# Keys of attention in three tiles of 128, with the left 64 of two head pairs worked in quarters of the array

## The chip, the cores and the metric

One core of a Trainium2 chip. The metric is the device time of one execution, in microseconds (us). Every kernel was run several times, alternating with the kernel before on the same chip.

In lines of the profile PE is TensorE (PEld its weight loads), DVE VectorE, ACT ScalarE, POOL GpSimd and SP SyncE; L486 is line 486 of that run's kernel; `[1.36 <-DVE ...]` is the idle time before an instruction and what ended it. PSUM is the memory where this kernel's products land; its tiles are banks of it, and a bank is written anew only after its last content was copied out. "Half clock" means a granted TensorE clock of 0.5.

## The reference, cut to what matters

```python
# q, k, v: (8 batches, 12 heads, 448 rows, 64)
q_n, k_n = rmsnorm(q, g_q), rmsnorm(k, g_k)
scores = (1 / 8) * q_n @ k_n.T                # 448 x 448 per head
attn = softmax(scores)
x = attn @ v                                  # bridged to (3584, 768)
h = x @ w_in                                  # 768 -> 2048
out = (h * sigmoid(h)) @ w_out                # 2048 -> 768, all float32
```

## The kernel before

Heads are taken in pairs, 48 pairs in all; a pair's 2 x 64 head columns fill 128 partitions. The 448 keys are cut into four tiles of 112. Scores have keys on partitions, so `e` needs no transpose for the weighted sums. Feed-forward products of finished batches are filled in between (`fill`), in two stretches per pair. Each batch of six pairs is an outer index `b`; feed-forward work starts small with the second batch and in full with the third.

```python
def transpose(n, name):                        # q shown; k alike, copied into kT times the gains
    t = ps.tile([P, S], F32, name="tr")        # one PSUM bank
    for j in range(J):                         # J = 4
        nc.tensor.transpose(t[:, ts(j, R)], rows[:, j, :], ident[0:R, 0:R])     # R = 112
    nc.scalar.copy(qT[n % 2], t)

def scores(n, half):
    for j in range(2 * half, 2 * half + 2):
        banks = ps.tile([P, 2, BANK], F32, name="sc", bufs=2)[0:R]
        for h in range(2):
            rows = ds(h * D, D)
            nc.tensor.matmul(banks[:, h, 0:S], kT[rows, ts(j, R)], qT[n % 2][rows, :], ...)
        for h in range(2):
            nc.scalar.activation(e[j][:, h, :], banks[:, h, 0:S], AF.Exp, scale=...)

def weigh(n, half):                            # for its two tiles and both heads
            nc.tensor.matmul(st["av"][ds(h * D, D), :], st["v"][:, h, j, :], e[j][:, h, :], ...)

def add_up(n, *chunks):                        # sum of e over tiles, for the row sums
    for j in chunks:
        nc.vector.tensor_tensor(out=t, in0=e[0] if j == 1 else t, in1=e[j], op=ALU.add)

for n in range(last + 2):                      # cut
    load(n + 3, "qk")
    scores(n, 0)
    weigh(n - 1, 1); load(n + 1, "v"); add_up(n - 1, 2, 3); unload(n - 1)   # ScalarE copies "av" out
    transpose(n + 1, "q")
    fill()
    divide_by_sums(n)                          # row sums, reciprocal, transfers
    scores(n, 1)
    weigh(n, 0)
    transpose(n + 1, "k")
    add_up(n, 1)
    fill()
    weights_in(n, 3)                           # queues two weight loads of 512 KB in the first 12 pairs
    normalise(n + 3)
```

## Time and profile before

| | |
|---|---|
| time, median (first runs) | 1458.72 us (1457.11 to 1459.0) |
| TensorE busy | 1429.4 of 1457.2 us |
| VectorE, ScalarE, GpSimd busy | 708.3, 540.4, 397.9 us |
| 13th pair's q transposes start | 126.1 us |
| from the 28th to the 48th pair's q transposes | 383.1 us |

The lines of the profile that carry this are in the prediction. The last two rows are marks: the first record of a pair's q transposes stands in every kernel's trace, so the times between two marks compare stretches. 126.1 us is the end of the stretch with little feed-forward work; from the 28th to the 48th pair the work repeats evenly, ten double pairs long.

### The profile page before, as it was taken

The page shows a single profiled execution, that of the slowest core. Times are in us where ns is not written, and L with a number is a line of the kernel's source. Part 1 is how long each engine was busy: PE and PEld are TensorE (multiplying, and loading weights), DVE is VectorE, ACT ScalarE, POOL GpSimd, SP SyncE. Part 2 cuts the span into 40 slices and gives each one's busy share as a digit, 9 for nine tenths or more (in the row PEclk, how much of TensorE's full clock was granted, in tenths as well). Part 3 has the DMA queues.
Part 4 walks back from the last instruction along what each step waited for, and adds up shares of the span by engine and source line. Part 5 has one row for each costly group of instructions (what it writes and reads, how often), then busy time and mean ns, then how long its engine had stood idle before and what let it go on. Part 6 is the DMA issues. An engine that isn't in the chain of part 4 may idle for free.

```text
span 1457.2 us, 14067 instructions
## 1 busy us (share of the span) xinstructions
PE 1429.4 (98%) x5057; PEld 699.0 (48%) x5057; DVE 708.3 (49%) x941; ACT 540.4 (37%) x907; POOL 397.9 (27%) x251
## 2 busy tenths in 40 slices
PE   8999999999999999999999999999999999999998
PEld 4333443434444444444444445555555555555554
DVE  5888776765645445654545687722222222222220
ACT  7876566645465465555555344300000000000000
POOL 6565443533323333333322054310000000000000
PEclk9999999999999999999999999999999999999999
DMA  6633344422232232223221167332222222222210
GB/s 188 174 93 112 91 127 134 126 67 73 64 98 74 61 105 67 70 67 99 68 66 66 58 181 246 123 98 78 83 83 80 81 81 83 80 85 84 85 58 25
DMA packets 124052, 137.67 MB, mean 94 GB/s; under 512 B 50372, under 2 KB 104644, under 8 KB 123972
## 3 DMA queue, kind: packets, MB, share of 16 engines
q1 hardware_dynamic: 123904, 136.62, 31.2%
q8 instruction: 42, 0.69, 0.2%
q14 instruction: 38, 0.31, 0.1%
q10 hardware_dynamic: 68, 0.05, 0.0%
HBM read 88.47 MB, written 41.29 MB: 89 GB/s over the span
## 4 chain that ended last, share of the span: by engine, by line
PE 84%; DVE 3%; DMA 1%; issue 1%; ACT 1%; POOL 0%; SPq 0%; ACTq 0%; DVEq 0%; POOLq 0%
PE mm L539 38%; PE sc L539 13%; PE sc L413 8%; PE av L429 8%; PE av L539 7%; PE tr L539 7%; PE tr L457 1%; PE tr L399 1%; PE tr L394 1%; DVE work L461 1%; DVE work L441 1%; DMA hidden<-stage 0%; DMA W<-in_moe_w_in_dram 0%; DVE rms L309 0%; DVE W L490 0%
## 5 line engine op out<-in xcount | busy, mean ns | idle before, releaser
L418 ACT ACTIVATE work<-sc,rms 112x448 f32<-112x448 f32 x384 | 211.9, 636 | 185.7 <-PE sc L413 149.3
L539 PE MATMUL mm<-x,W 128*128 128x448 f32 x648 | 261.0, 542 | 1.2 <-DVE stage L490 1.1
L315 POOL TENSOR_TENSOR rms<-rms,minus_half 112x16 f32<-112x16 f32 (+1 forms) x49 | 176.3, 3599 | 255.5 <-DVE rms L311 254.8
L539 PE MATMUL mm<-sums_x,W 128*128 128x448 f32 x480 | 194.6, 542 | 2.7 <-DVE parts L490 1.8
L413 PE MATMUL sc<-work 64*112 64x448 f32 x768 | 172.4, 568 | 2.2 <-ACT work L403 0.8
L539 PEld LDWEIGHTS mm<-x,W 128*128 128x128 f32 x648 | 118.6, 190 | 107.6 <-issue 98.4
L429 PE MATMUL av<-work,rows 112*64 112x448 f32 x768 | 165.6, 552 | 0.0
L441 DVE TENSOR_TENSOR work<-work 112x896 f32<-112x896 f32 x144 | 157.9, 1097 | 1.8
L559 POOL TENSOR_TENSOR parts<-parts,stage 128x448 f32<-128x448 f32 (+1 forms) x37 | 42.2, 1139 | 336.4 <-DVE parts L490 336.4
L539 PEld LDWEIGHTS mm<-sums_x,W 128*128 128x128 f32 x480 | 88.0, 190 | 81.7 <-issue 72.3
L413 PEld LDWEIGHTS sc<-work 64*112 64x112 f32 x768 | 61.7, 174 | 104.6 <-issue 78.5
L429 PEld LDWEIGHTS av<-work,rows 112*64 112x64 f32 x768 | 46.7, 136 | 106.6 <-issue 100.1
L559 POOL TENSOR_TENSOR parts<-parts,W 128x384 f32<-128x384 f32 x9 | 8.9, 994 | 307.5 <-DVE parts L490 307.5
L461 DVE RECIPROCAL work<-tr 128x448 f32<-128x448 f32 x25 | 73.9, 2956 | 37.6 <-PE tr L457 37.5
L490 DVE TENSOR_TENSOR stage<-mm,parts 128x448 f32<-128x448 f32 (+1 forms) x59 | 36.3, 616 | 86.0 <-PE mm L539 57.0
L546 ACT COPY stage<-mm 128x448 f32<-128x448 f32 (+1 forms) x34 | 17.8, 524 | 155.7 <-PE mm L539 146.0
L670 ACT ACTIVATE stage<-stage 128x896 f32<-128x896 f32 x64 | 58.4, 945 | 36.7 <-DVE stage L490 35.7
L539 PE MATMUL mm<-W,work 128*128 128x384 f32 x204 | 68.6, 486 | 0.0
L539 PE MATMUL sc<-W,work 128*128 128x384 f32 x192 | 64.5, 486 | 0.0
L405 DVE TENSOR_SCALAR work<-tr,gains 128x448 f32<-128x448 f32 x36 | 24.6, 684 | 73.7 <-PE tr L399 73.7
L309 DVE TENSOR_REDUCE rms<-qn 112x8 f32<-112x512 f32 x49 | 33.4, 682 | 48.9 <-ACT qn L308 48.8
L319 POOL TENSOR_TENSOR qn<-rows,rms 112x512 f32<-112x512 f32 x46 | 55.1, 1198 | 3.6
(158 smaller groups left out, 1789.5 us busy)
## 6 DMA issues: line engine op xcount, KB each, us to landing
hidden<-stage SPq DMA_DIRECT2D x64, 448.0 KB, 2.8
work<-hidden SPq DMA_DIRECT2D x7, 2048.0 KB, 9.3
x<-hidden SPq DMA_DIRECT2D x7, 2048.0 KB, 8.8
W<-in_moe_w_in_dram SPq DMA_DIRECT2D x24, 512.0 KB, 4.7
rows<-in_moe_w_out_dram SPq DMA_DIRECT2D x32, 384.0 KB, 3.5
rows<-in_q_dram SPq DMA_DIRECT2D x48, 224.0 KB, 3.5
rows<-in_k_dram SPq DMA_DIRECT2D x48, 224.0 KB, 4.2
rows<-in_v_dram SPq DMA_DIRECT2D x48, 224.0 KB, 2.7
```

The lines of the kernel that those rows point to most:

```text
L309: nc.vector.tensor_reduce(out=rms[:, i], in_=t, axis=AX.X, op=ALU.add)
L315: nc.gpsimd.tensor_tensor(out=flat, in0=flat, in1=half, op=ALU.pow)
L319: engine.tensor_tensor(out=by_head, in0=rows["q"], in1=factor, op=ALU.mult)
L413: nc.tensor.matmul(banks[:, h, 0:S], kT[rows, ts(j, R)], qT[n % 2][rows, :], start=True, stop=True,)
L418: nc.scalar.activation(e[j][:, h, :], banks[:, h, 0:S], AF.Exp, scale=rms[n % 4][:, 1, h, j : j + 1])
L429: nc.tensor.matmul(st["av"][ds(h * D, D), :], st["v"][:, h, j, :], e[j][:, h, :], start=(j == 0), stop=(j == J - 1),)
L441: nc.vector.tensor_tensor(out=t, in0=e[0] if j == 1 else t, in1=e[j], op=ALU.add)
L461: nc.vector.reciprocal(out=r[0], in_=t)
L490: nc.vector.tensor_tensor(out=out, in0=a, in1=b, op=ALU.add)
L539: nc.tensor.matmul(t, self.left(name, s), self.right(name, s), start=s == ends[0], stop=s == ends[1])
L559: nc.gpsimd.tensor_tensor(out=u2, in0=u2, in1=p5, op=ALU.add)
L670: nc.scalar.activation(t, t, AF.Silu)
```

## The change

Three tiles of 128 keys instead of four of 112 leave 64 keys of each head. Those of an even pair and of the odd pair after it share one tile. Its four products (two pairs, two heads) have 64 rows and 64 columns each, so they fit the four quarters of the array at once, for scores and for weighted sums. For this the loads of k and v are split, the weighted sums of two pairs need two PSUM banks at once ("end0" and "end1", which also take the transposes and row sums in turn), and odd iterations do the weighted sums before their scores.

```diff
+    def scores(n, *units):
+        for j in units:
+            banks = ps.tile([P, 2, BANK], F32, name="sc", bufs=2)
+            members = [n] if j < LEFT else [n, n + 1]
+            size = P // len(members)
+            for i, m in enumerate(members):
+                for h in range(2):
+                    rows = ds(h * D, D)
+                    nc.tensor.matmul(banks[ds(i * size, size), h, 0:S],
+                        kT[rows, ds(j * P + i * size, size)], qT[m % 2][rows, :], ...)
 ... (cut)
+    def add_up(n, *units):
+        for j in units:
+            rows = ds(0, P) if j < LEFT else ds(n % 2 * z.LEFT, z.LEFT)
+            nc.vector.tensor_tensor(out=t[rows], in0=e[0] if j == 1 else t[rows], in1=e[j][rows], ...)
 ... (cut; the loop)
-        if n <= last:
-            scores(n, 0)
+        if n <= last and (n < 2 or not odd):
+            scores(n, 0, 1)
         if n > 0:
-            weigh(n - 1, 1)
+            weigh(n - 1, LEFT - 1)
+            if odd:
+                weigh(n, LEFT)
             load(n + 1, "v")
-            add_up(n - 1, 2, 3)
+            add_up(n - 1, LEFT - 1)
+            if odd:
+                add_up(n - 1, LEFT)
             unload(n - 1)
+        if n > 1 and odd:
+            scores(n, 0, 1)
 ... (cut: transpose q, fill, divide_by_sums)
-            scores(n, 1)
+            scores(n, LEFT - 1)
+            if n > 0 and not odd:
+                scores(n, LEFT)
 ... (cut)
-            weigh(n, 0)
+            weigh(n, 0, 1)
 ... (cut: transpose k)
             add_up(n, 1)
+            if odd:
+                add_up(n, LEFT)
```

More of the change, by code (lines that the diff above doesn't have):

```diff
@@ L43, in __init__ @@
         self.REST = self.S - self.FULL * self.P
+        self.KEYS = self.S // self.P
+        self.LEFT = self.S - self.KEYS * self.P
+        assert 2 * self.LEFT == self.P and self.NPAIR % 2 == 0
         assert 2 * self.D == self.P and self.J * self.R == self.S and 2 * self.REST == self.P
@@ L204 @@
     ring = const.tile([P, 7 * n], F32, name="rows")
-    slots = [ring[0:R, ds(i * n, n)] for i in range(7)]
+    slots = [ring[:, ds(i * n, n)] for i in range(7)]
     rings = {"q": slots[0:2], "k": slots[2:5], "v": slots[5:7]}
@@ L217, in load, with load_plain @@
         for name in names:
-            order = "p j h d" if name == "k" else "p h j d"
             t = rings[name][n % len(rings[name])]
-            t = t.rearrange(f"p ({order[2:]}) -> {order}", h=2, j=J)
-            nc.sync.dma_start(
-                t, sources[name][b, ts(hp, 2)].rearrange(f"h (p j) d -> {order}", j=J)
-            )
-            state[n][name] = t if name != "k" else t.rearrange("p j h d -> p h j d")
+            source = sources[name][b]
+            if name == "q":
+                t = t[0:R].rearrange("p (h j d) -> p h j d", h=2, j=J)
+                nc.sync.dma_start(t, source[ts(hp, 2)].rearrange("h (p j) d -> p h j d", j=J))
+                state[n][name] = t
+                continue
+            size = z.KEYS * 2 * D
+            if name == "k":
+                main = t[:, 0:size].rearrange("p (j h d) -> p j h d", j=z.KEYS, h=2)
+                order = "p j h d"
+            else:
+                main = t[:, 0:size].rearrange("p (h j d) -> p h j d", h=2, j=z.KEYS)
+                order = "p h j d"
+            keys = source[ts(hp, 2), 0 : z.KEYS * P].rearrange(f"h (p j) d -> {order}", j=z.KEYS)
+            nc.sync.dma_start(main, keys)
+            state[n][name] = t if name == "k" else main
+            if hp % 2 == 0:
+                left = t[:, ds(size, 2 * D)].rearrange("p (h d) -> p h d", h=2)
+                for i in range(2):
+                    rest = source[ts(hp + i, 2), z.KEYS * P : z.S].rearrange("h p d -> p h d")
+                    nc.sync.dma_start(left[ds(i * z.LEFT, z.LEFT)], rest)
+                state[n][name + "left"] = left
+    def load_plain(state, n):
+        b, hp = pairs[n]
+        for name in "qkv":
+            t = rings[name][n % len(rings[name])][0:R]
+            t = t.rearrange("p (h j d) -> p h j d", h=2, j=J)
+            nc.sync.dma_start(t, sources[name][b, ts(hp, 2)].rearrange("h (p j) d -> p h j d", j=J))
+            state[n][name] = t
     load(state, 0, "qk")
     load(state, 1, "qk")
-    g1 = const.tile([1, 2, D], F32, name="g1")
+    room = Room(nc, const, w_in, z)
+    g1, both = (
+        room.rest[0:1, ds(room.rest.shape[1] - (i + 1) * 2 * D, 2 * D)].rearrange(
+            "p (two d) -> p two d", two=2
+        )
+        for i in range(2)
+    )
     gains = const.tile([P, 1], F32, name="gains")
@@ L233 @@
         nc.scalar.dma_start(g1[:, i, :], g.rearrange("(one d) -> one d", one=1))
-    room = Room(nc, const, w_in, z)
     for n in range(2):
@@ L248 @@
     most = const.tile([1, 1], F32, name="most")
-    both = const.tile([1, 2, D], F32, name="both")
     wide = [g1[:, i : i + 1, :].to_broadcast([1, 2, D]) for i in range(2)]
@@ L274 @@
     normal = [const.tile([R, J, 2, D], F32, name=f"qn{i}") for i in range(2)]
-    rms = [const.tile([R, 2, 2, J], F32, name=f"rms{i}") for i in range(4)]
-    normalise_rows(
-        nc, z, state[0], normal[0], normal[1].rearrange("p j h d -> p h j d"), rms[0], minus_half,
-        nc.vector, together=False,
-    )
+    rms = [const.tile([P, 4 * J], F32, name=f"rms{i}") for i in range(4)]
+    for t in rms:
+        nc.gpsimd.memset(t, 1.0)
+    spare = const.tile([P, 2 * J * D], F32, name="squares")
+    normalise_rows(nc, z, state[0], normal[0], spare, rms[0], minus_half, nc.vector, together=False)
     def arm():
         own = [dict(st) for st in state]
+        plain = [dict() for st in state]
         r = copy.copy(room)
@@ L287, in arm @@
             tc=tc, nc=nc, z=z, pairs=pairs, state=own, load=lambda *a: load(own, *a), room=r,
-            ring=ring, w_out=w_out, normal=(normal, rms), ident=ident, ones=ones,
+            plain=(plain, lambda n: load_plain(plain, n)), spare=spare, ring=ring, w_out=w_out, normal=(normal, rms), ident=ident, ones=ones,
             minus_half=minus_half, gains=gains, out=out,
@@ L303, in normalise_rows, with q_squares, k_squares, root @@
     by_head = normal.rearrange("p j h d -> p h j d")
-    names = (("q", by_head), ("k", squares))
-    for part in ([0, 1],) if together else ([0], [1]):
-        for i in part:
-            name, t = names[i]
-            nc.scalar.activation(t, rows[name], AF.Square)
-            nc.vector.tensor_reduce(out=rms[:, i], in_=t, axis=AX.X, op=ALU.add)
-        flat = rms[:, ds(part[0], len(part))].rearrange("p i h j -> p (i h j)")
+    nq = 2 * z.J
+    nk = 2 * (z.KEYS + ("kleft" in rows))
+    def q_squares():
+        nc.scalar.activation(by_head, rows["q"], AF.Square)
+        nc.vector.tensor_reduce(
+            out=rms[0 : z.R, 0:nq].rearrange("p (h j) -> p h j", h=2), in_=by_head, axis=AX.X,
+            op=ALU.add,
+        )
+    def k_squares():
+        size = nk * z.D
+        nc.scalar.activation(squares[:, 0:size], rows["k"][:, 0:size], AF.Square)
+        nc.vector.tensor_reduce(
+            out=rms[:, ds(nq, nk)], in_=squares[:, 0:size].rearrange("p (n d) -> p n d", n=nk),
+            axis=AX.X, op=ALU.add,
+        )
+    def root(flat):
         nc.vector.tensor_scalar(
@@ L313, in normalise_rows, with scale @@
         )
-        half = minus_half[0 : z.R].to_broadcast([z.R, len(part) * 2 * z.J])
+        half = minus_half[0 : flat.shape[0]].to_broadcast(list(flat.shape))
         nc.gpsimd.tensor_tensor(out=flat, in0=flat, in1=half, op=ALU.pow)
-        if 0 in part:
-            factor = rms[:, 0].rearrange("p h (j one) -> p h j one", one=1)
-            factor = factor.to_broadcast([z.R, 2, z.J, z.D])
-            engine.tensor_tensor(out=by_head, in0=rows["q"], in1=factor, op=ALU.mult)
+    def scale():
+        factor = rms[0 : z.R, 0:nq].rearrange("p (h j one) -> p h j one", h=2, one=1)
+        factor = factor.to_broadcast([z.R, 2, z.J, z.D])
+        engine.tensor_tensor(out=by_head, in0=rows["q"], in1=factor, op=ALU.mult)
+    q_squares()
+    if together:
+        k_squares()
+        root(rms[:, 0 : nq + nk])
+        scale()
+    else:
+        root(rms[0 : z.R, 0:nq])
+        scale()
+        k_squares()
+        root(rms[:, ds(nq, nk)])
 def store(nc, out, z, column, o, m0, *queues):
@@ L337, in bounded @@
 def bounded(
-    ctx, tc, nc, z, pairs, state, load, room, ring, normal, w_out, ident, ones, minus_half,
-    gains, out,
+    ctx, tc, nc, z, pairs, state, load, plain, room, spare, ring, normal, w_out, ident, ones,
+    minus_half, gains, out,
 ):
@@ L364, in bounded @@
     parts = mem.tile([P, 2 * S], F32, name="parts")
-    work = mem.tile([P, 17 * S + 2 * J * D], F32, name="work")
+    work = mem.tile([P, 17 * S + z.LEFT], F32, name="work")
     qT0, qT1, kT, e0, e1, e2, e3, es0, es1, r0, r1 = divided(
-        work, S, S, S, 2 * S, 2 * S, 2 * S, 2 * S, 2 * S, 2 * S, S, S
+        work, S, S, S + z.LEFT, 2 * S, 2 * S, 2 * S, 2 * S, 2 * S, 2 * S, S, S
     )
@@ L370, in bounded @@
     normal, rms = normal
-    squares = work[0:R, ds(17 * S, 2 * J * D)].rearrange("p (h j d) -> p h j d", h=2, j=J)
-    e = [t[0:R].rearrange("p (h s) -> p h s", h=2) for t in (e0, e1, e2, e3)]
-    es = [t[0:R].rearrange("p (h s) -> p h s", h=2) for t in (es0, es1)]
+    e = [t.rearrange("p (h s) -> p h s", h=2) for t in (e0, e1, e2, e3)]
+    es = [t.rearrange("p (h s) -> p h s", h=2) for t in (es0, es1)]
+    LEFT = z.KEYS
     def xT(b, c):
@@ L381, in normalise, with av, tr @@
             normalise_rows(
-                nc, z, state[n], normal[n % 2], squares, rms[n % 4], minus_half,
+                nc, z, state[n], normal[n % 2], spare, rms[n % 4], minus_half,
                 nc.gpsimd if n > 1 else nc.vector,
             )
+    def av(n):
+        return "end0" if (n // 2 + n) % 2 == 0 else "end1"
+    def tr(n):
+        return "end1" if av(n) == "end0" else "end0"
     def transpose(n, name):
@@ L389, in transpose @@
             return
-        t = ps.tile([P, S], F32, name="tr")
+        t = ps.tile([P, BANK], F32, name=tr(max(n - 1, 0)))
         if name == "q":
@@ L394, in transpose @@
                 nc.tensor.transpose(t[:, ts(j, R)], rows[:, j, :], ident[0:R, 0:R])
-            nc.scalar.copy(qT[n % 2], t)
+            nc.scalar.copy(qT[n % 2], t[:, 0:S])
         else:
-            rows = state[n]["k"].rearrange("p h j d -> p j h d")
-            for j in range(J):
-                nc.tensor.transpose(
-                    t[:, ts(j, R)], rows[:, j].rearrange("p h d -> p (h d)"), ident[0:R, 0:R]
-                )
-            if n < 2 * z.NPAIR:
-                nc.scalar.activation(kT, t, AF.Copy, scale=gains)
-            else:
-                nc.vector.tensor_scalar_mul(out=kT, in0=t, scalar1=gains)
@@ L407, in scores @@
-    def scores(n, half):
-        for j in range(2 * half, 2 * half + 2):
-            banks = ps.tile([P, 2, BANK], F32, name="sc", bufs=2)[0:R]
-            for h in range(2):
-                rows = ds(h * D, D)
-                nc.tensor.matmul(
-                    banks[:, h, 0:S], kT[rows, ts(j, R)], qT[n % 2][rows, :],
-                    start=True, stop=True,
-                )
-            for h in range(2):
-                nc.scalar.activation(
-                    e[j][:, h, :], banks[:, h, 0:S], AF.Exp, scale=rms[n % 4][:, 1, h, j : j + 1]
-                )
@@ L422, in weigh @@
-    def weigh(n, half):
-        st = state[n]
-        if half == 0:
-            st["av"] = ps.tile([P, S], F32, name="av")
-        for j in range(2 * half, 2 * half + 2):
-            for h in range(2):
-                nc.tensor.matmul(
-                    st["av"][ds(h * D, D), :],
-                    st["v"][:, h, j, :],
-                    e[j][:, h, :],
-                    start=(j == 0),
-                    stop=(j == J - 1),
-                )
-    def add_up(n, *chunks):
-        t = es[n % 2]
-        for j in chunks:
-            nc.vector.tensor_tensor(out=t, in0=e[0] if j == 1 else t, in1=e[j], op=ALU.add)
+            columns = (z.KEYS + ("kleft" in state[n])) * P
@@ new lines, in transpose @@
+            for j in range(columns // P):
+                nc.tensor.transpose(t[:, ts(j, P)], state[n]["k"][:, ts(j, P)], ident)
+            if n < 2 * z.NPAIR:
+                nc.scalar.activation(kT[:, 0:columns], t[:, 0:columns], AF.Copy, scale=gains)
+            else:
+                nc.vector.tensor_scalar_mul(out=kT[:, 0:columns], in0=t[:, 0:columns], scalar1=gains)
+    def scores(n, *units):
[6 more added lines that the diff above has]
+                    rows = ds(h * D, D)
+                    nc.tensor.matmul(
+                        banks[ds(i * size, size), h, 0:S],
+                        kT[rows, ds(j * P + i * size, size)],
+                        qT[m % 2][rows, :],
+                        start=True, stop=True,
+                    )
+            for h in range(2):
+                column = 2 * (J + j) + h
+                nc.scalar.activation(
+                    e[j][:, h, :], banks[:, h, 0:S], AF.Exp,
+                    scale=rms[n % 4][:, column : column + 1],
+                )
@@ new lines, in weigh @@
+    def weigh(n, *units):
+        for j in units:
+            members = [n] if j < LEFT else [n - 1, n]
+            size = P // len(members)
+            for i, m in enumerate(members):
+                if j == (LEFT if m % 2 else 0):
+                    state[m]["av"] = ps.tile([P, BANK], F32, name=av(m))[:, 0:S]
+            for i, m in enumerate(members):
+                rows = ds(i * size, size)
+                for h in range(2):
+                    v = state[n]["v"][:, h, j] if j < LEFT else state[n - 1]["vleft"][rows, h]
+                    nc.tensor.matmul(
+                        state[m]["av"][ds(h * D, D), :], v, e[j][rows, h, :],
+                        start=(j == (LEFT if m % 2 else 0)),
+                        stop=(j == (LEFT - 1 if m % 2 else LEFT)),
+                    )
@@ L443, in unload @@
+    def add_up(n, *units):
+        t = es[n % 2]
+        for j in units:
+            rows = ds(0, P) if j < LEFT else ds(n % 2 * z.LEFT, z.LEFT)
+            nc.vector.tensor_tensor(
+                out=t[rows], in0=e[0] if j == 1 else t[rows], in1=e[j][rows], op=ALU.add
+            )
     def unload(n):
@@ L453, in sums @@
     def sums(members, width):
-        t = ps.tile([P, S], F32, name="tr") if members[0] >= z.NPAIR else bank(S)
+        beside = members[-1] + 1
+        t = ps.tile([P, BANK], F32, name=tr(beside))[:, 0:S] if members[0] >= z.NPAIR else bank(S)
         for h in range(2):
@@ L457, in sums @@
                 nc.tensor.matmul(
-                    t[ds(h * D + i * width, width), :], ones[0:R, 0:width], es[n % 2][:, h, :],
+                    t[ds(h * D + i * width, width), :], ones[:, 0:width], es[n % 2][:, h, :],
                     start=True, stop=True,
@@ L509, in bounded @@
     alone = False
-    order = ["mm", "mm", "sc", "sc", "tr", "av"]
+    order = ["mm", "mm", "sc", "sc", tr(last + 1), av(last)]
     def bank(n):
@@ L520, in bank @@
             return ps.tile([P, BANK], F32, name=name, bufs=2)[:, 0:n]
-        return ps.tile([P, S], F32, name=name)[:, 0:n]
+        return ps.tile([P, BANK], F32, name=name)[:, 0:n]
     class Seven:
@@ L829, in bounded @@
         ends = b > 0 and b % 2 == 0 and hp == 0
+        odd = n % 2 == 1
         load(n + 3, "qk")
-        if n <= last:
-            scores(n, 0)
+        if n <= last and (n < 2 or not odd):
+            scores(n, 0, 1)
         if n > 0:
-            weigh(n - 1, 1)
+            weigh(n - 1, LEFT - 1)
+            if odd:
+                weigh(n, LEFT)
             load(n + 1, "v")
-            add_up(n - 1, 2, 3)
+            add_up(n - 1, LEFT - 1)
+            if odd:
+                add_up(n - 1, LEFT)
             unload(n - 1)
@@ L862, in bounded @@
         if n <= last:
-            weigh(n, 0)
+            weigh(n, 0, 1)
         if n == 0:
             transpose(n + 1, "q")
-            transpose(n + 1, "k")
-        if b > 0:
+            scores(n, LEFT)
+        if b > 0 or n == 0:
             transpose(n + 1, "k")
@@ L908, in general @@
 def general(
-    ctx, tc, nc, z, pairs, state, load, room, ring, normal, w_out, ident, ones, minus_half,
-    gains, out,
+    ctx, tc, nc, z, pairs, state, load, plain, room, spare, ring, normal, w_out, ident, ones,
+    minus_half, gains, out,
 ):
+    state, load = plain
     P, D, R, J, S = z.P, z.D, z.R, z.J, z.S
@@ L1075, in general @@
     for n, (b, hp) in enumerate(pairs):
-        if n > 1:
-            load(n)
+        load(n)
         normalise(n)
```

## The prediction

> **What bounds the kernel now.** I read the page's busy line first, then the chain that ended last (as shares and in order of time), then the groups by line, the waits of TensorE, and a table of busy time by stretch.
>
> ```profile
> PE 1429.4 (98%) x5057; PEld 699.0 (48%) x5057; DVE 708.3 (49%) x941; ACT 540.4 (37%) x907; POOL 397.9 (27%) x251
> ...
> PE 84%; DVE 3%; DMA 1%; issue 1%; ACT 1%; POOL 0%; SPq 0%; ACTq 0%; DVEq 0%; POOLq 0%
> ```
>
> TensorE is busy nearly all the time and carries the chain. "Busy" can hide stalls, because the ends of pipelined matmuls are modelled, so I take durations from the chain in order of time. Columns: start us, us, what, records.
>
> ```profile
> 407.58 0.89 PE tr L457 x8
> 408.47 1.69 PE sc L413 x8
> 410.16 1.65 PE av L429 x8
> 411.81 0.53 PE tr L399 x4
> 412.35 5.28 PE mm L539 x14
> 417.62 1.69 PE sc L413 x8
> ```
>
> This is half a pair of heads: row sums (L457), two key tiles of scores for both heads (L413), two of weighted sums (L429), a transpose, then feed-forward products that fill in. Plain products set the scale: 14 records in 5.28 us, so one 448-column record takes a slot of 0.377 us; a product has two records. The 8 score records are four products (two tiles, two heads) in 1.69 us, 4 slots and 0.18 us: the two heads run side by side. The weighted sums likewise: 4 slots and 0.14 us. The row sums have 8 records in 0.89 us, 2 slots and 0.14 us: four products at once, so this kernel already runs four column strips together. The rest of each block I read as the cost of changing the array's shape.
>
> ```profile
> L418 ACT ACTIVATE work<-sc,rms 112x448 f32<-112x448 f32 x384 | 211.9, 636 | 185.7 <-PE sc L413 149.3
> L413 PE MATMUL sc<-work 64*112 64x448 f32 x768 | 172.4, 568 | 2.2 <-ACT work L403 0.8
> L429 PE MATMUL av<-work,rows 112*64 112x448 f32 x768 | 165.6, 552 | 0.0
> L441 DVE TENSOR_TENSOR work<-work 112x896 f32<-112x896 f32 x144 | 157.9, 1097 | 1.8
> ```
>
> ScalarE's exponentials wait for TensorE's scores (149.3 us) and the matmuls almost never wait for them. The waits of TensorE are few:
>
> ```profile
> PE mm L457 <- DVE work L441: 4.0, 3, 3.1
> PE tr L399 <- DVE work L461: 3.9, 3, 1.8
> ...
> PE tr L457 <- ACT work L395: 1.7, 2, 0.9
> PE tr L457 <- DVE work L441: 1.5, 2, 1.1
> ```
>
> By stretch (columns: window; length, then busy PE, PEld, DVE, ACT, POOL with counts; clock, DMA share, GB/s):
>
> ```profile
> 20.00:60.00 40.00, 36.48 (x168) 13.04 (x164) 32.06 (x41) 30.81 (x59) 26.16 (x13) 0.88 0.56 158
> ...
> 100.00:140.00 40.00, 37.85 (x180) 14.41 (x177) 34.75 (x48) 30.46 (x58) 19.58 (x10) 1.00 0.45 131
> ...
> 400.00:800.00 400.00, 399.80 (x1523) 173.52 (x1522) 204.83 (x258) 212.87 (x336) 126.26 (x68) 1.00 0.25 76
> ```
>
> The first twelve pairs (to about 135 us) have little feed-forward work; VectorE and ScalarE are 75 to 87% busy there, hardly less than TensorE. The other 36 pairs (about 19 us each, to 826 us) have half-idle helpers. After 826 us no attention is left and the change touches nothing.
>
> **What the Trainium skill says.** "TensorEngine Tiling (Array Packing)", Tiling Modes, Key Properties: tiles run independently, but changing the tiling mode drains the engine. The trace agrees: the first record after a change starts 0.467 us after the one before instead of 0.376, and the second record is another 0.02 us late with 32 weight columns, 0.05 with 64, 0.09 with 112, since the first weight load isn't hidden.
> Same page, Tiling Modes: 64 by 64 gives four independent tiles. No record of before has that shape; two row halves and four column strips are each seen at once.
> Same page, Restrictions and Gotchas, Gotcha 1: row tiles must write different PSUM banks at the same time. The diff obeys it: quarter scores go to one bank per head, quarter weighted sums to one bank per pair ("end0", "end1").
> "TensorE: Matmul & The Clock Gate", LDWEIGHTS: load time follows the columns. The trace: 0.137 us for 64, 0.173 for 112, 0.190 for 128. So key tiles of 128 lengthen only the exposed first load.
>
> **The change part by part.** Per pair, four tiles of 112 keys become three of 128 plus half a tile shared with the next pair.
>
> 1. Slots. Two pairs now take 2 x (4 + 4) = 16 tile units (scores and weighted sums), each of 2 slots, 0.752 us. After: 14. From the blocks: a two-tile block is 1.69 (scores) or 1.65 (sums); a one-tile block is 1.69 - 0.75 = 0.94 or 1.65 - 0.75 = 0.90. Before: 4 x 1.69 + 4 x 1.65 = 13.36 us. After, by the loop's order: scores 2 x 1.69 + 2 x 0.94 = 5.26; sums 2 x 0.90 + 2 x 1.65 = 5.10; the two quarter blocks, each a change of shape of its own, 2 x 0.90 = 1.80 (estimate: as a sums block with 64 weight columns). Total 12.16, so 1.20 us less per two pairs, 24 times: -28.8 us. Without the two added changes of shape it would be -36.
> 2. Wider first load in four score blocks, about 0.013 us each (0.190 - 0.173, rounded down): +1.2 us.
> 3. K transposes: 8 of 112 columns (0.096 us each) become 7 of 128 (about 0.109): nothing.
> 4. Row sums: one product per head and pair still, with 128 rows: nothing. Single pairs (the last two of every odd batch) have their reciprocal of 2.96 us in the same bank as the K transposes that follow. From the last row-sum record to the transpose TensorE has 3.8 us of work now, which just covers 0.6 + 2.96. In an odd iteration one tile (0.75) goes, so it waits about 0.55 us; four such: +2.2 us.
> 5. Banks. In odd iterations the transposes of q use the bank of the previous pair's sums, so they wait for ScalarE's copy out of it. Between lie 1.7 us of scores. Going through the 24 odd iterations of the trace and asking how late ScalarE's earlier work ends there (Silu, squares), I find 2.1 us of waits, nearly all in three of them: +2.0 us.
> 6. Exponentials: 8 per pair become 7 on average, 48 x 0.55 us = 26 us of ScalarE's time. It isn't the bound, so this is worth nothing by itself; it keeps the first twelve pairs from becoming ScalarE-bound.
> 7. Adds on VectorE: still three per pair, the third with 64 rows but the same 896 columns, so no time saved. At even iterations only one instead of two runs before the row sums, which eases the waits of 4.0 and 1.5 us above: -1 us. VectorE's unchanged load against a shorter TensorE around pairs 11 to 13 takes back about 1.5 us.
> 8. Start: two more DMA issues of about 0.65 us ahead of pair 1, one more bank wait in iteration 0: +0.7 us.
>
> Sum: -28.8 + 1.2 + 2.2 + 2.0 - 1 + 1.5 + 0.7 = -22.2 us, 1436. I take 1435, as a little of items 4 and 5 may overlap with existing waits.
>
> **The rivals.**
> (a) The quarters don't all run at once (two by two): a quarter unit costs 4 slots, 0.75 us more, 48 times, 36 us back: about 1470. For it: no quarter is in the trace. Against: four strips run at once in the row sums, and banks are kept apart. One in twelve.
> (b) A helper becomes the bound in the first twelve pairs: ScalarE loses as much as TensorE, but VectorE loses nothing and is at 87% in one stretch. Then those six double pairs save nothing and the time is about 1442. Against: half of its stalls now come from the adds of item 7.
> (c) The change of shape costs less between kindred shapes (half rows to quarters), or the 3.1 us stall near 54 us, which is followed by some 5 us at half clock (0.88 in that stretch), vanishes with the earlier row sums. That is worth 3 to 6 us: about 1428.
> (d) The bank sharing waits more often than item 5 has it, since the feed-forward work shifts: up to 8 us more, about 1443.
>
> **Range and chances.** The saving in slots is the surest term; two thirds of the spread come from changes of shape, bank waits and the start. Eight times in ten: 1426 to 1446. The line of 2% is at 1429.5; being below it needs (c) without (b) and (d): 0.2. Slower by 2% (over 1487.8) needs (a) with new stalls: 0.03. Within 2%: 0.77.
>
> **What would show it.** Right: scores and weighted sums still have 768 records each (48 pairs x 3 tiles x 2 heads x 2 records, and 24 quarter units x 4 products x 2), but the quarter blocks in the chain last about 0.90 us for 8 records, and a double pair loses 1.20 us. The exponentials are 336 and still 0.55 us apart. New waits stand at the q transposes for the copy out of the bank, and at the K transposes for the reciprocal, some 2 us each. Wrong: quarter blocks of 1.6 us (rival a); TensorE waiting over 10 us in total in the first 140 us more than now (b); waits for the copy over 5 us (d). In 400 to 800 us, where helpers have room, the saving must be nearly the slots' alone: 0.5 us per pair.

## The result, and the profile after

The time is 1447.45 us median of four runs (1445.15 to 1449.98), ratio 0.9925 with a 95% interval of 0.9905 to 0.9945: within 2%, and 1.5 us outside the top of the range. A ratio is the mean time of one kernel's runs over that of the other's of the same rounds, so not quite the ratio of the medians. The gain is 11 us instead of 24.

The chain in order of time, after the change, for one even and one odd iteration (start us, us, what, records):

```profile
405.30 1.86 PE sc L486 x12
407.17 1.65 PE end L512 x8
408.82 0.48 PE end L470 x3
...
414.56 1.82 PE end L512 x12
416.38 1.70 PE sc L486 x8
...
423.89 0.95 PE sc L486 x4
...
426.50 0.60 PE end L470 x4
...
427.13 0.75 DVE work L474
```

L486 are scores, L512 weighted sums, L470 the transposes of K, L474 VectorE's copy of them. Further down, L542 are row sums, L465 the transposes of q, L624 feed-forward products, L523 adds, L546 the reciprocal of the row sums. A score block with one full tile and the quarters (12 records) takes 1.86 us: 4 slots of 0.377 us and two changes of shape. So the quarters run four at once, and 0.94 + 0.90 = 1.84 was expected. The like block of weighted sums takes 1.82. Added up by record starts, a double pair's attention takes 14.90 us against 16.03 before: 1.13 us less, where the prediction had 1.15 with its second item. The core of the prediction held. The last line shows what did not: the chain leaves TensorE for VectorE.

The page after the change, busy time and chain:

```profile
PE 1407.0 (97%) x5033; PEld 682.5 (47%) x5033; DVE 710.1 (49%) x941; ACT 510.5 (35%) x859; POOL 388.2 (27%) x255
...
PE 83%; DVE 5%; issue 1%; ACT 1%; DMA 0%; POOL 0%; SPq 0%; DVEq 0%; ACTq 0%; POOLq 0%
```

TensorE is busy 22.4 us less, but the span is only 10.4 us shorter: idle time rose from 1457.2 - 1429.4 = 27.8 to 1446.8 - 1407.0 = 39.8 us. VectorE's share of the chain rose from 3 to 5%. TensorE's waits, with total us, times and longest:

```profile
PE mm L624 <- DVE parts L575: 5.6, 7, 1.4
PE end L470 <- DVE work L546: 4.7, 5, 2.3
PE mm L542 <- DVE work L523: 4.7, 2, 3.5
PE end L465 <- ACT x L528: 3.5, 2, 2.2
PE end L542 <- ACT work L466: 3.3, 2, 1.7
PE mm L624 <- DVE stage L575: 2.0, 2, 1.4
PE mm L624 <- ACT stage L631: 2.0, 3, 0.7
```

The first line and the two last are feed-forward products waiting for a PSUM bank to be emptied. Together they are 9.6 us. Before, these two lines stood for them, 3.6 us, and the one for ScalarE was not there:

```profile
PE mm L539 <- DVE stage L490: 1.8, 3, 0.9
PE mm L539 <- DVE parts L490: 1.8, 1, 1.8
```

The second line after the change is the transposes of K behind the reciprocal (3.9 us before), the third the row sums behind the adds (4.0 before), the fourth the transposes of q behind the copy out of the shared bank (new), the fifth the row sums behind the copy of q (1.7 before). The adds by shape:

```profile
L523 DVE TENSOR_TENSOR work<-work 128x896 f32<-128x896 f32 x96 | 105.8, 1102 | 0.0
...
L523 DVE TENSOR_TENSOR work<-work 64x896 f32<-64x896 f32 x48 | 55.1, 1149 | 1.7
```

The 64-row adds cost VectorE as much as those of 128 rows, as predicted. Here is where they stand on VectorE, at the end of an odd iteration (start us, us, engine, line):

```profile
427.13 0.75 DVE L474 TENSOR_SCALAR work<-end,gains 128x512 f32<-128x512 f32 x1 [5.96 <-PE end L470]
427.79 2.21 DVE L523 TENSOR_TENSOR work<-work 128x896 f32<-128x896 f32 x2
430.03 0.62 DVE L575 TENSOR_TENSOR stage<-mm,stage 128x448 f32<-128x448 f32 x1
430.57 0.62 DVE L575 TENSOR_TENSOR parts<-mm,stage 128x448 f32<-128x448 f32 x1
430.71 0.64 PE L624 MATMUL mm<-sums_x,W 128*128 128x448 f32 x1 [1.36 <-DVE stage L575]
```

VectorE copies K (L474), does both adds (L523), and only then empties the two finished product banks (L575). There are two such banks, so TensorE stands for 1.36 us. Before, one add stood here and two at the start of the iteration, and the bank was reached 1.6 us after the copy of K began, not 2.9:

```profile
430.69 0.68 DVE L405 TENSOR_SCALAR work<-tr,gains 128x448 f32<-128x448 f32 x1 [6.55 <-PE tr L399]
431.29 1.08 DVE L441 TENSOR_TENSOR work<-work 112x896 f32<-112x896 f32 x1
432.29 0.62 DVE L490 TENSOR_TENSOR stage<-mm,stage 128x448 f32<-128x448 f32 x1
```

By marks: the 13th pair's q transposes start at 127.1 us, 1.0 us later than before, so the first twelve pairs gained nothing in sum. The way there was uneven: 3.0 us behind at the fourth pair's mark, 1.5 us ahead at the twelfth's. From the 28th to the 48th pair 376.8 us pass, 6.3 us less, where ten double pairs at 1.13 would make 11.3.

### The profile page after: what moved, and what is told of

Its sections match the earlier page's. It is cut to its first block, busy times and chain, and to the rows that moved or that the text cites. A ratio compares the mean times of both kernels' runs of the same rounds, so it can differ in the third digit from the quotient of the medians. Undisturbed runs are those within 1.5% of the kernel's fastest.

```text
span 1446.8 us, 14152 instructions
## 1 busy us (share of the span) xinstructions
PE 1407.0 (97%) x5033; PEld 682.5 (47%) x5033; DVE 710.1 (49%) x941; ACT 510.5 (35%) x859; POOL 388.2 (27%) x255
## 4 chain that ended last, share of the span: by engine, by line
PE 83%; DVE 5%; issue 1%; ACT 1%; DMA 0%; POOL 0%; SPq 0%; DVEq 0%; ACTq 0%; POOLq 0%
PE mm L624 38%; PE end L624 14%; PE sc L624 14%; PE sc L486 7%; PE end L512 7%; DVE work L523 1%; PE end L542 1%; PE end L465 1%; DVE work L546 1%; PE end L470 1%; DVE work L474 0%; DVE W L575 0%; DVE parts L575 0%; DVE stage L575 0%; DVE sums_x L572 0%
## 5 line engine op out<-in xcount | busy, mean ns | idle before, releaser
L624 PE MATMUL mm<-x,W 128*128 128x448 f32 x648 | 261.0, 542 | 4.9 <-DVE parts L575 2.0
L494 ACT ACTIVATE work<-sc,rms 128x448 f32<-128x448 f32 x336 | 187.0, 634 | 148.1 <-PE sc L486 92.7
L365 POOL TENSOR_TENSOR rms<-rms,minus_half 128x14 f32<-128x14 f32 (+3 forms) x49 | 168.3, 3435 | 246.7 <-DVE rms L361 231.5
L624 PE MATMUL mm<-sums_x,W 128*128 128x448 f32 x480 | 196.5, 547 | 5.6 <-DVE parts L575 3.6
L624 PEld LDWEIGHTS mm<-x,W 128*128 128x128 f32 x648 | 118.4, 190 | 111.8 <-issue 96.1
L486 PE MATMUL sc<-work 64*128 64x448 f32 (+1 forms) x768 | 160.9, 582 | 2.1 <-ACT work L472 1.3
L523 DVE TENSOR_TENSOR work<-work 128x896 f32<-128x896 f32 x144 | 160.9, 1118 | 1.7
L512 PE MATMUL end<-work,rows 128*64 128x448 f32 (+1 forms) x768 | 152.2, 561 | 0.0
L624 PEld LDWEIGHTS mm<-sums_x,W 128*128 128x128 f32 x480 | 87.9, 191 | 87.1 <-issue 70.4
L486 PEld LDWEIGHTS sc<-work 64*128 64x128 f32 (+1 forms) x768 | 53.7, 176 | 102.4 <-issue 84.2
L546 DVE RECIPROCAL work<-end 128x448 f32<-128x448 f32 x25 | 73.9, 2956 | 37.3 <-PE end L542 37.2
L512 PEld LDWEIGHTS end<-work,rows 128*64 128x64 f32 (+1 forms) x768 | 38.3, 135 | 101.5 <-issue 90.7
L575 DVE TENSOR_TENSOR stage<-mm,parts 128x448 f32<-128x448 f32 (+1 forms) x59 | 36.3, 615 | 87.6 <-PE mm L624 49.4
L624 PE MATMUL mm<-W,work 128*128 128x384 f32 x204 | 68.6, 486 | 0.0
L624 PE MATMUL sc<-W,work 128*128 128x384 f32 x192 | 64.5, 486 | 0.0
L624 PE MATMUL end<-W,work 128*128 128x384 f32 x192 | 64.5, 486 | 0.0
L474 DVE TENSOR_SCALAR work<-end,gains 128x512 f32<-128x512 f32 (+1 forms) x36 | 24.6, 685 | 63.8 <-PE end L470 63.7
```

The costliest lines, as they stand in the source:

```text
L365: nc.gpsimd.tensor_tensor(out=flat, in0=flat, in1=half, op=ALU.pow)
L474: nc.vector.tensor_scalar_mul(out=kT[:, 0:columns], in0=t[:, 0:columns], scalar1=gains)
L486: nc.tensor.matmul(banks[ds(i * size, size), h, 0:S], kT[rows, ds(j * P + i * size, size)], qT[m % 2][rows, :], start=True, stop=True,)
L512: nc.tensor.matmul(state[m]["av"][ds(h * D, D), :], v, e[j][rows, h, :], start=(j == (LEFT if m % 2 else 0)), stop=(j == (LEFT - 1 if m % ...
L523: nc.vector.tensor_tensor(out=t[rows], in0=e[0] if j == 1 else t[rows], in1=e[j][rows], op=ALU.add)
L546: nc.vector.reciprocal(out=r[0], in_=t)
```

## The experiments

Theory A: in the even stretch the gain is lost to the order on VectorE just shown. Rival B: VectorE's load as such takes it. For the first twelve pairs theory C blames ScalarE, theory D a loop through the loads; the prediction's own view was TensorE, with VectorE as rival. "Change" stands for the changed kernel at 1447.45 us. A single profile's marks scatter by 1 to 2 us before the 28th pair; the stretch from the 28th to the 48th repeats to 0.1 us where nothing in it was edited (383.1 with a mere edit of load order to the kernel before).

One source of the scatter can be read from the traces. Their clock records show stretches of 3.4 us, or of twice that, in which TensorE was granted half its clock; each 3.4 us can cost TensorE up to 1.7 us (an estimate: half the stretch). Before the 13th mark the kernel before has three such lengths (at 19.4 us, and 53.5 us, twice as long), the change four (11.6, 28.6, 55.9, 117.4), and the experiments, in the order below, 3, 4, 4, 2, 1, 3, 2, 2, 1, 0 and 1. So a mark that moves by a few us is an edit's doing only where these stretches are alike. The changed kernel itself was not run again beside the experiments; the kernel before was, and its medians were 1458.3 to 1459.3 us.

**The add moved behind the feed-forward stretch**

```diff
             add_up(n, 1)
-            if odd:
-                add_up(n, LEFT)
 ...
         elif not ends:
             fill()
+        if n <= last and odd:
+            add_up(n, LEFT)
         weights_in(n, 3)
```

> Edit: in odd iterations the add of the 64 left rows moves from before the second stretch of feed-forward work to behind it; nothing else changes. Theory A (half of the missing gain is TensorE waiting for product banks, because VectorE now does the K copy and two adds, some 2.9 us, before it empties a finished bank): TensorE's waits on feed-forward products for the DVE lines that empty banks fall from 8.5 us to under 4, and the time falls by 4 to 7 us, to about 1441-1443. Rival B (those waits come from VectorE's total load, not from the order): the waits move elsewhere and the time stays within 2 us of 1447.

Measured: 1439.89 us (1439.17 to 1440.63), ratio 0.9867 (0.9853 to 0.9882): 7.6 us below the change, a little more than the 4 to 7 expected. TensorE's waits in that run:

```profile
PE end L542 <- ACT work L466: 4.6, 2, 3.0
...
PE mm L624 <- DVE stage L575: 0.9, 3, 0.4
...
PE mm L624 <- DVE parts L575: 0.4, 1, 0.4
```

The bank waits (the last two lines) fell from 9.6 to 1.3 us, their line for ScalarE is gone, and the even stretch is 10.9 us shorter than before instead of 6.3. That is 1.09 per double pair, nearly all that the blocks promised. Theory A holds there.

**The adds of the left rows taken out**

```diff
-            if odd:
-                add_up(n - 1, LEFT)
 ...
-            if odd:
-                add_up(n, LEFT)
```

> Edit: the adds of the 64 left rows are left out altogether (the result is wrong on purpose: the row sums miss those keys). VectorE loses 48 adds of 1.1 us. Theory A: about the same as moving the add (1441-1443), a little better in the first twelve pairs: 1438-1442. Rival B (VectorE's load is what holds the first twelve pairs and the product banks): clearly better than moving it, 1435 or less.

Measured: 1434.75 us (1433.67 to 1438.43), ratio 0.9838. By the time alone this is rival B's forecast (1435 or less), and theory A's (1438 to 1442) missed. The marks say where: the even stretch is 11.4 us shorter than before, hardly more than with the add moved, so there it was nearly all order. From the 14th to the 28th pair it is 8.6 us shorter than before, against 5.4 with the add moved; VectorE also prepares weights and sums there, and rival B has a part. The profile was of a run of 1438.24 us, 3.5 above the median, so where the rest of the 5 us lies was not seen. The 13th pair's mark came at 127.9, with half-clock stretches within 0.4 us of the change's: in this profile the adds of the left rows do not hold the first twelve pairs.

**All scores in quarters**

```diff
-            members = [n] if j < LEFT else [n, n + 1]
+            members = [n, n] if j < LEFT else [n, n + 1]
```

> Edit: every score product is issued as two products of 64 keys, so that all scores run in quarters of the array and the quarter block of the shared keys needs no change of shape after the score block. Same slots if four quarters run at once. If so and a change of shape costs what was read from the blocks (0.09 us, and 0.05 instead of 0.10 us for the first weight load): per two pairs one change less (0.14) and four first loads shorter by 0.05, together 0.34 us, 24 times 8 us where TensorE is the bound: 1440-1443. If quarters run only two at a time, every score block doubles: 48 x 3 x 0.75 = 108 us slower.

Measured: 1440.84 us (1439.22 to 1441.43), ratio 0.9873. The chain of that run:

```profile
402.55 1.67 PE sc L486 x16
...
413.42 1.50 PE sc L486 x16
```

The block of one tile and the shared keys took 1.86 us and takes 1.67; the one behind the quarter sums took 1.70 and takes 1.50, which is four slots with no change of shape at all. So a change of shape, with the exposed first load, costs 0.19 to 0.20 us at a score block. The even stretch is 4.4 us shorter than with the change, 0.44 per double pair where 0.34 was expected. The waits on banks stayed (5.2 and 2.8 us in the lines for VectorE), so this gain is separate from that of the first experiment.

**The quarter scores issued twice**

```diff
-            for i, m in enumerate(members):
+            for i, m in list(enumerate(members)) * (2 if j == LEFT else 1):
```

> Edit: the four quarter products of each shared score block are issued twice (the second time over the first, so the result stays right). It measures a quarter block's slots by themselves. If four quarters run at once, a block gets 2 slots longer, 0.75 us in the chain (1.86 becomes 2.61 for the block of one tile and the quarters), and the time grows by 24 x 0.75 = 18 us, less a few us if TensorE's waits shrink: 1460-1466. If two run at a time: 1.5 us per block and about 1484.

Measured: 1460.26 us (1458.6 to 1460.74), ratio 1.0009. The block in the chain:

```profile
409.10 2.62 PE sc L486 x20
```

2.62 - 1.86 = 0.76 us for four more products: four at once, and rival (a) of the prediction falls. In the even stretch the time grows by 7.5 us against the change, 0.75 in each double pair, so no wait there took any of it in. The whole grew by 13 us and not 18: the 13th mark moved by less than 0.1 us, where 6 x 0.75 = 4.5 us more were due. This profile has two half-clock stretches fewer before it (up to 3.4 us). 1460.26 is the low end of what was expected; how much shrinking waits took in is not shown.

**q's transposes behind the first feed-forward stretch in odd iterations**

```diff
-        if n > 0:
+        if n > 0 and (not odd or b == 0):
             transpose(n + 1, "q")
 ...
             fill()
+        if odd and b > 0:
+            transpose(n + 1, "q")
```

> Edit: in odd iterations from the seventh pair on, the transposes of q come after the first stretch of feed-forward work instead of before it, so they no longer wait for the copy out of the bank of the weighted sums. Of the 3.5 us of such waits in the profile, 1.4 to 1.9 us lie there (near 230 us); the 2.2 us near 25 us stay. Expected: 1 to 2 us faster, 1445-1447, unless the single pairs' row sums then wait for the copy of q (up to 4 x 0.5 us), which would cancel it.

Measured: 1449.25 us (1448.06 to 1453.42), ratio 0.9938: no gain. The wait for the copy fell from 3.5 to 2.2 us, as meant. But the row sums' waits for the copy of q rose from 3.3 to 4.7 us and those of products on VectorE from 7.6 to 10.4. The wait moved.

**The copy of q ahead of the copy out of the bank, in even iterations**

```diff
-            unload(n - 1)
+            if odd or ends:
+                unload(n - 1)
 ...
             transpose(n + 1, "q")
+            if not odd and not ends:
+                unload(n - 1)
```

> Edit: in even iterations ScalarE copies q's transposes before it empties the bank of the weighted sums, instead of after. Theory C (in the first twelve pairs ScalarE's chain from the K copy to the q copy is longer than TensorE's work beside it, and since an even iteration lost 0.75 us of weighted sums, all of that became a wait of the row sums for the q copy: 3.3 us in two waits): those two waits shrink by 0.5 us each and iterations gain 0.5 us there; the mark of the 13th pair's q transposes moves from 127.1 to about 125.5, the time to 1445-1446. Rival (VectorE holds the first twelve pairs): no change, since its order stays.

To see what is at stake, ScalarE and TensorE in the second half of the first twelve pairs. Before the change:

```profile
110.70 0.63 ACT L403 ACTIVATE work<-tr,gains 128x448 f32<-128x448 f32 x1 [0.71 <-PE tr L399]
...
113.08 1.72 PE L429 MATMUL av<-work,rows 112*64 112x448 f32 x8
...
117.00 1.05 PE L457 MATMUL tr<-work,ones 112*32 112x448 f32 x8 [0.90 <-ACT work L395]
```

After it:

```profile
109.84 0.69 ACT L472 ACTIVATE work<-end,gains 128x512 f32<-128x512 f32 x1 [1.06 <-PE end L470]
...
112.28 0.97 PE L512 MATMUL end<-work,rows 128*64 128x448 f32 x4
...
116.30 0.96 PE L542 MATMUL end<-work,ones 128*32 128x448 f32 x8 [1.74 <-ACT work L466]
```

The row sums here share their bank with q's transposes and wait until ScalarE has copied those. From ScalarE's K copy to that point (weight opening, squares, four exponentials, two copies) 6.3 us pass before (117.00 - 110.70), 6.5 after. TensorE's work beside it lost one tile of weighted sums (1.72 to 0.97 us), but ScalarE's did not get shorter. So the wait of the row sums grew from 0.90 to 1.74 us: this half of the even iteration's gain became a wait. From the tenth pair's mark to the twelfth's, two iterations, 20.7 us pass before and 20.1 after, 0.6 instead of 1.13 us less.

Measured: 1446.03 us (1444.48 to 1447.05), ratio 0.9914 (0.9901 to 0.9927), whose interval overlaps with the change's. The two waits fell from 3.3 to 2.9 us in sum, the two iterations from 20.1 to 19.7 us, the two before them from 20.5 to 20.0; neither profile has a half-clock stretch in these. The 13th pair's mark at 125.3 proves nothing: this profile has one half-clock stretch fewer before it, and it was 2.4 us ahead at the fourth pair's mark, where the change's profile had had two and this one none. The direction and the place are those of theory C, but the effect is small and the time alone does not prove it.

**Iteration 1 in the order of the other odd ones**

```diff
-        if n <= last and (n < 2 or not odd):
+        if n <= last and not odd:
 ...
-        if n > 1 and odd:
+        if odd:
```

> Edit: iteration 1 runs in the order of the other odd ones, weighted sums first and its scores after, so that the copy out of the bank comes before its four exponentials on ScalarE. In the profile the q transposes near 25 us wait 2.2 us for that copy and the scores near 20 us wait 1.25 us for the K copy. Expected: the first wait goes and the second is filled, 2 to 3 us faster at the mark of the third pair, and if nothing later swallows it, 1444-1446. If the first twelve pairs are held by a helper, it is swallowed and the mark of the 13th pair stays at 127.

Measured: 1445.98 us (1443.46 to 1448.37), ratio 0.9918: 1.5 us by the medians, within the scatter. In the profile the 2.2 us wait for the copy is gone (the longest is 1.3), the fourth pair's mark comes 2.3 us earlier, and the 13th pair's at 122.4. Some of this is clock: the change's profile had half-clock stretches near 12 and 117 us that this one has not. Against the profile of the first experiment, which has none near 12 us either, the fourth mark is 1.2 us earlier. Near 117 us, in the change's profile, a wait of 1.74 us is followed, from 117.3 us, by a score block of 3.35 instead of 1.86 us. In the change's four runs such stretches can be seen in the granted clock: 1445 and 1446 us at 0.997, 1449 and 1450 us at 0.994 and 0.993.

**All four helpful edits together**

> All helpful edits together: the add behind the second stretch, all scores in quarters, the copy order in even iterations, and iteration 1 as the other odd ones. Each alone: -7.6 and -6.6 measured, -1.5 and -2 expected. If they touch different waits they add: 1429-1432. If waits take each other's place: 1434-1437.

Measured: 1435.42 us (1432.63 to 1437.6), ratio 0.9847. In the even stretch the gains add nearly in full: 15.1 us less than before, 1.51 per double pair (1.09 and 0.44 from the first and third experiment). Over the whole they do not (12.0 us where the single gains add to 17.1), which is the forecast for waits that take each other's place; the 13th mark is at 125.2.

**Loads of q and k queued ahead of the weight loads**, in the kernel before and in the changed one

```diff
-        load(n + 3, "qk")
+        if n == 0:
+            load(3, "qk")
 ...
+        load(n + 4, "qk")
         weights_in(n, 3)
```

> Edit to the kernel BEFORE the change: the loads of q and k of a later pair are queued just ahead of the two weight loads (1 MB) of the same iteration instead of just behind them. Theory D (in the first twelve pairs the end is not set by TensorE but by a closed loop: row sums, reciprocal, six transfers on SyncE's queue, then weight loads, then q and k loads, their squares on ScalarE, exponentials, two copies, row sums again): two iterations take 20.7 us near 100 us though TensorE's own work is about 19.2; with the loads first, k lands some 4 us earlier and the loop opens, 1 to 1.5 us less per two pairs: the mark of the 13th pair's q transposes moves from 126.1 to 120-123 and the time to 1453-1456. Rival (TensorE is the bound there too, as the prediction had it): no change beyond 1 us.

> The same edit to the changed kernel. Theory D: TensorE's own work there is about 18.1 us per two pairs against 20.1 in the profile, so more is to be had than before the change: the mark of the 13th pair moves from 127.1 to 118-122, the time to 1438-1442. The gain of the change over the kernel before with the same edit is then nearer to the 1.13 us per two pairs read from the blocks. Rival: as above, no change.

Measured: the kernel before 1452.18 us (1451.38 to 1453.01), ratio 0.9951, its 13th pair at 121.8; the changed kernel 1441.72 us (1440.83 to 1443.4), ratio 0.9884, its 13th pair at 119.8. The marks are as theory D had them, and the times too but for 0.8 us, but its reason fails: near 100 us two iterations still take 20.7 and 20.1 us, to 0.1 us as without the edit, so no loop through the loads sets them. In the kernel before the gain lies at one place near 50 us. Without the edit:

```profile
54.40 1.71 PE L457 MATMUL mm<-work,ones 112*32 112x448 f32 x6 [3.05 <-DVE work L441]
56.05 3.33 PE L413 MATMUL sc<-work 64*112 64x448 f32 x8
```

The kernel before with the loads first:

```profile
53.23 0.95 PE L457 MATMUL mm<-work,ones 112*32 112x448 f32 x6 [0.58 <-DVE work L441]
54.12 1.76 PE L413 MATMUL sc<-work 64*112 64x448 f32 x8
```

With k late, its squares on ScalarE and the sums and adds on VectorE behind them were late, the row sums waited 3.05 us, and the array then ran at half clock (3.33 us for a block of 1.76). This was there before the change and stayed with it (3.5 us, 1.4 with the loads first). In the changed kernel this place makes 3.6 of the 7.2 us by which the 13th mark moved; the rest goes with the half-clock stretches near 12, 29 and 117 us, of which that profile has none. It does not explain the missing gain of the change: with the same edit on both sides the change gains 10.5 us by the medians, about as without.

**The four edits and the loads first**

> The four edits of the run of all helpful edits, and the loads first. If the loop was what held the first twelve pairs, this takes 4 to 8 us more off than those four: 1427-1431, more than 2% below the kernel before. If a helper is the bound there: 1434-1436 as without it.

Measured: 1428.86 us (1428.04 to 1432.03), ratio 0.9796 (0.9782 to 0.981), correct. It is below both kernels; whether by 2% of the kernel before is unclear, as the interval spans 0.98. The single edits' gains (7.6, 6.6, 1.4, 1.5 and 5.7) add to 22.8; together they make 18.6. In its first twelve pairs VectorE is now busy 34.38 of 40 us (20 to 60 us), and the row sums wait 7.3 us for its adds in three waits. By this VectorE is the next to hold them, which no run tested.

## Why the prediction was wrong

- Item 1 and 2, slots and changes of shape: right. 1.13 us per double pair against 1.15, four quarters at once, no rival (a).
- Item 3, K transposes: right (0.48 and 0.60 us in place of twice 0.53).
- Item 4, reciprocal of the single pairs: right in kind. Three new waits of 0.45 to 0.48 us stand at odd single iterations (near 133, 353 and 577 us); predicted were four of 0.55 each.
- Item 5, shared bank: 3.5 us in two waits against 2.0. One, in a later iteration (near 232 us), was 1.36 us; the other, 2.2, was in iteration 1. There I had asked only how late Silu and squares end on ScalarE, and missed that iteration 1 keeps its scores, and so four exponentials, ahead of the copy.
- Item 6, exponentials: 30 us less on ScalarE, 26 reckoned. That this is worth nothing by itself was not tested.
- Item 7 is the step that failed: "Adds on VectorE: still three per pair [...] so no time saved." The count was right and the place was not looked at. Moving one add from the start of an odd pair's successor to the end of the odd iteration put 2.2 us of adds, in place of 1.1, behind the K copy and in front of the emptying of product banks. That cost 7.6 us, as the first experiment showed by moving it. The closing sentence, that from 400 to 800 us "the saving must be nearly the slots' alone", was wrong for this reason: 0.31 us per pair were saved there, and 0.55 once the add was moved. (Its 0.5 us per pair is not the slots alone, which would be 0.75, but items 1 and 2 together, 1.15 for two pairs, rounded down.) The expected ease of the row sums (-1 us) did not come either; those waits stayed at 5.5 us in sum.
- Item 8, the start (0.7 us): not to be told. The first mark came 0.8 us later, but in the changed kernel and its edits it lies anywhere from 9.2 to 10.6 us.
- The first twelve pairs: the prediction let 6 x 1.15 us through but for 1.5 on VectorE. They gained nothing in the profile. From 14 us to the 13th mark TensorE's waits grew from 7.1 to 12.4 us, which is most of what the blocks saved there (6 x 1.13). Of these 5.3 us, 2.2 are the wait in iteration 1, and 1.6 the row sums' wait for ScalarE's copy, which in two iterations grew by what TensorE saved; the rest is spread, 0.7 of it over the row sums' wait for VectorE's adds. The prediction's text said that ScalarE "loses as much as TensorE"; over two pairs it does, but its exponentials leave the odd iterations, while the half iteration that sets the pace kept all its work. Rival (b) had the effect right and named VectorE, where the larger part was ScalarE's; its own sign, over 10 us more of waits, did not come. What the half-clock stretches took of it varies from run to run; I can't give each us its cause, and that ScalarE's order holds these pairs is shown only in small part by the edit of the copy order.
- Rival (d) came at a size of 1.5 us more than item 5; rival (c) as hoped for did not come by itself; the third experiment shows that the change of shape was worth taking out. (Its "some 5 us at half clock" are 6.8 in the trace, 53.5 to 60.3 us, 0.9 of them inside the stall; the 0.88 of that window also holds part of a stretch near 20 us.)

## What to carry to other kernels

Work taken off the busiest engine paid here only where each buffer that it reached sooner was also freed sooner. So, for every instruction that a change moves on a helper, look at what stands behind it in that engine's order, above all the copy that empties a matmul's bank. Count per iteration and per half iteration, not per pair: a helper that gets lighter on average may give nothing if the stretch that sets the pace keeps its load. And if a small shape must be mixed in, see whether its neighbours can take the same shape.

## What the Trainium skill lacked or had wrong

- "TensorEngine Tiling (Array Packing)", Tiling Modes: it says that a change of tiling mode drains the engine, without a figure. Here it costs 0.09 us and the part of the first weight load that no longer overlaps; taking it out saved 0.19 to 0.20 us per score block of 448 columns. Four independent 64 by 64 tiles are confirmed: four products in 0.76 us.
- "TensorE: Matmul & The Clock Gate", Part 1: it puts the fall to half clock after an idle window of about 3.4 us. Here half-rate blocks came with shorter waits: 3.33 for 1.76 us after one of 3.05 us, and 3.35 for 1.86 us after one of 1.74 us. The half clock of the first began at 53.5 us, inside the wait, which ended at 54.4. With the first wait cut to 0.58 us by the edit of the loads, the half clock there was gone. Not every wait of that length does it: in the kernel before one of 1.80 us near 237 us was followed by full clock.
